# The second product of a mixture layer made to follow half a token tile behind the first, in place of a whole tile

## The chip, the core and the metric

One core of a Trainium2 chip runs the kernel. The core has TensorE (PE, with its weight loads shown apart as PEld), VectorE (DVE), ScalarE (ACT), GpSimd (POOL) and SyncE (SP, which here only issues transfers, from one queue in order). The metric is the device time of one execution in microseconds (us), lower is better; runs are compared by their median.

## The reference, cut to what matters

An attention stage makes `x`, a first gated layer (MoE 1) changes it, and the second layer (MoE 2) makes the output. Only MoE 2 is touched:

```python
def _moe2_ref(x, w_in, w_out):      # x (2304, 512), w_in (512, 2048), w_out (2048, 512)
    h = x @ w_in
    sp = np.where(h > 20.0, h, np.log1p(np.exp(np.minimum(h, 20.0))))
    g = h * np.tanh(sp)
    return (g @ w_out).astype(np.float32)
```

So there is a first product (`x @ w_in`), an elementwise function (Mish) of it, and a second product (`g @ w_out`).

## The kernel before, in words

Every operand is split into a high and a low part, so each product is made of three matmuls (high by high, high by low, low by high: lines 1644 to 1646 for the first product, 1657 to 1659 for the second).

**Tiles.** MoE 2 runs twice over the tokens, once for each half `h` of the 2048 hidden features, since only half of the weights fits. Within a half it goes over five token tiles `t`: four of 512 tokens and one with the remaining 256 (`REST`). In the half `h = 1` the tiles come in reverse. A tile has two phases, `d = 0` and `d = 1`; each takes two of the half's four quads of features, a quad being 256 features. A phase is half a tile's first product.

**A phase** (`phase`) makes seven sub-products P1 to P7 (a Strassen-like scheme), each of 12 matmuls with 256 columns (`product`), in the order 1, 5, 6, 2, 7, 3, 4. They go into four PSUM tiles: hX, hZ and one of hY0 and hY1. After P1, ACT copies hX into y (line 1781), on which P6 then accumulates. After P5, ACT copies hZ into v (line 1784). After P6, DVE adds y and v into hZ (line 1787), and only then may P7 accumulate on y. After P7, DVE adds y and v into `c22` (line 1793), and only then may P4 accumulate on y. P2, P3 and P4 are copied out by ACT (lines 1790, 1797, 1800). The results stand in two SBUF buffers, hsA (c11 and c22) and hsB (c12 and c21).

**Mish.** `mish` takes one such buffer through DVE (1664), ACT (1665), DVE (1666), ACT (1667 and 1668), DVE (1669 and 1670); `put_g` then writes the high part with ACT (1677) and the low part with DVE (1678) into `g2`. This is called the chain below; each phase has two, eA from hsA and eB from hsB. eA serves token parts and feature blocks 0 and 1 of `g2`, eB blocks 2 and 3.

**The second product** is cut into units `m2out(t, f, a)`: feature block `f` (0 to 7 of the half; 0 to 3 come from phase 0, 4 to 7 from phase 1) by token part `a` (0 to 3; 0 and 1 in `REST`). A unit is three matmuls with 512 columns, adding to the PSUM tile `po[a]`. Below "f0a2" stands for the unit with f = 0 and a = 2. f0a0 and f0a1 need eA of their phase; f0a2, f0a3, f1a0 and f1a1 need eB. After the eighth block `finish` moves `po[a]` out: in `h = 0` an ACT copy (1695) and a store to `pd`; in `h = 1` a load of `pd` into one of two buffers `r` (1700), a DVE addition (1701) and a store of the output (1703).

**Order.** The code deals the units of an earlier tile out between the products of a phase (`go(share[k])`). It is only a wish: the framework's scheduler reorders the instructions of every engine by its own estimate of when each can start. So the order that counts is that of the built program.

**Beside that** run, in `h = 0`, 16 jobs that prepare the other half's weights (POOL 190, DVE 198, 201, 205 and 231, ACT 228, stores by SP). SP also loads the next tile's `xu` (1572), the blocks of `w_out` (`load_o2`, line 1559) and the second half of `w_in`.

Of the kernel before, what the change touches and what calls it, by code (L numbers as in the profile page):

```python
# [59 lines left out]
def attn_moe_kernel(  # L60
# [14 lines left out]
    B, H, S, D = q.shape  # L75
# [17 lines left out]
    NQ = KF2 // 4  # L93
# [66 lines left out]
    for n in range(B * NU1):  # L160
        i = n % NRING
# [1317 lines left out]
    if True:  # L1479
# [21 lines left out]
        for b in range(B - 1):  # L1501
# [11 lines left out]
            if b:  # L1513
# [3 lines left out]
                    lambda i, d, b=b: park_o2((b - 1) * per + i, d), 19000.0,  # L1517
# [40 lines left out]
        def load_o2(h, j):  # L1558
            SP.dma_start(out=wo_at[j].bitcast(F32), in_=wd2[h * 8 + j].rearrange("p z f -> p (z f)"))
# [90 lines left out]
        def m2out(t, f, a):  # L1650
            q, fi = divmod(f, 2)
            T, part = divmod(a, 2)
            ts = slice(part * 128, (part + 1) * 128)
            gh, gl = (g2[:, q, BLK[fi, T] if t < B else fi, z, ts] for z in range(2))
            w = wo_at[f].rearrange("p (z f) -> p z f", z=2)
            p = po[a]
            PE.matmul(p, lhsT=gh, rhs=w[:, 0, :], start=(f == 0), stop=False)  # L1657
            PE.matmul(p, lhsT=gh, rhs=w[:, 1, :], start=False, stop=False)  # L1658
            PE.matmul(p, lhsT=gl, rhs=w[:, 0, :], start=False, stop=(f == 2 * NQ - 1))  # L1659
# [88 lines left out]
        n_y = [0]  # L1748

        def phase(t, quads, units, follow, share):  # L1750

            hsA, hsB = hs_at
# [55 lines left out]
        prev = None  # L1808
        for s, (h, t) in enumerate(order):
            after = order[s + 1] if s + 1 < len(order) else None  # L1810
            for d in range(NQ // 2):
                quads = (2 * d, 2 * d + 1)
                units = []
                if prev is not None:
                    ph, pt = prev
                    for q in quads:
                        for f in (2 * q, 2 * q + 1):
                            for a in range(4 if pt < B else 2):
                                units.append(lambda f=f, a=a, pt=pt: m2out(pt, f, a))

                def follow(i, d=d):
                    if d != NQ // 2 - 1 or after is None or after[1] == t:
                        return
                    if t < B:
                        load_x2(after[1], i)
                    elif i:
                        load_x2(after[1], 4 - i)

                n = 4 if t == REST else 7
                per = len(units) / n  # L1830
                share = [round(per * (k + 1)) - round(per * k) for k in range(n)]
                if after is None:
                    share = [1] * 7
                phase(t, quads, units, follow, share)
                if after is not None and after[0] != h:
                    for q in quads:
                        load_wi(q)
                if prev is None and d == 0:
                    for j in range(2, 8):
                        load_o2(0, j)  # L1840
                if prev is not None and prev[0] != h:
                    for q in quads:
                        for f in (2 * q, 2 * q + 1):
                            load_o2(1, f)
            if prev is not None:
                for a in range(4 if prev[1] < B else 2):
                    finish(prev[0], prev[1], a)
            prev = (h, t)
        for a in range(4):
            for f in range(2 * NQ):  # L1850
                m2out(prev[1], f, a)
            finish(prev[0], prev[1], a)
        assert not side
# [37 lines left out]
```

## Time and profile before

| what | value |
|---|---|
| median of 3 runs | 1016.59 us (1015.89 to 1020.15) |
| the profiled execution's own time | 1020.45 us |
| its span, first to last instruction | 1018.6 us |
| mean granted TensorE clock, share of full speed | 0.981 |
| PE busy | 988.6 us, 97% of the span |
| DVE busy | 681.2 us, 67% |
| ACT busy | 579.0 us, 57% |
| MoE 2 in the trace | about 623 us to the end |

Busy times are sums over instructions of one engine. Matmuls are pipelined, so a record of a matmul overlaps the next one's; how long a matmul occupies TensorE is read from the distance of two starts. The profiled execution is 3.86 us slower than the median of the runs; a prediction made against its trace has to be moved to the runs' level.

### The profile page before, as it was taken

To read this page: it belongs to the slowest core of one execution; us is meant where nothing else is said; L and a number is where in the kernel's file an instruction comes from. 1 tells how busy PE (TensorE), PEld (TensorE's weight loads), DVE (VectorE), ACT (ScalarE), POOL (GpSimd) and SP (SyncE) were. 2 spreads that over 40 slices of the span, in tenths; PEclk is the share of its full clock that TensorE was granted. 3 is DMA by queue.
4 is the path that set the end of the run, shared out by engine and by line. 5 is a ranking of instruction groups with operands and counts; after the bars stand their busy time and mean duration, and the time that the engine had idled before them with its cause. 6 is when DMAs were issued, how large, how long until landed. Compare 5 with 4: busy or idle time off the path is not lost. (4 is left out here: it accounts for less than half of the span.)

```text
span 1018.6 us, 20914 instructions
## 1 busy us (share of the span) xinstructions
PE 988.6 (97%) x8188; PEld 923.3 (91%) x8188; DVE 681.2 (67%) x1034; ACT 579.0 (57%) x1292; POOL 296.3 (29%) x319
## 2 busy tenths in 40 slices
PE   9989799999999999999999999899999999999998
PEld 7889698898999999999999999798988889988986
DVE  5845776776776567765688732897888545766664
ACT  6547677656656455755545533766566454745452
POOL 5846573662412324010254311142433100000000
PEclk9689799999999999999999999999999999999999
DMA  8378765689443484442464726866758794362503
GB/s 201 105 187 220 212 207 167 212 275 300 125 152 106 125 275 129 145 125 82 161 220 138 186 92 199 307 221 239 256 211 218 297 352 126 104 200 78 157 17 129
DMA packets 159090, 184.86 MB, mean 181 GB/s; under 512 B 68368, under 2 KB 121360, under 8 KB 158480
## 3 DMA queue, kind: packets, MB, share of 16 engines
q1 hardware_dynamic: 155296, 179.87, 55.9%
q0 software_dynamic: 3696, 3.67, 1.6%
q8 instruction: 64, 1.05, 0.4%
q14 instruction: 34, 0.28, 0.1%
HBM read 132.38 MB, written 51.12 MB: 180 GB/s over the span
## 5 line engine op out<-in xcount | busy, mean ns | idle before, releaser
L1293 PE MATMUL ps_m<-R 128*128 128x288 f32 (+2 forms) x768 | 235.8, 308 | 6.0 <-ACT R L228 3.6
L1294 PE MATMUL ps_m<-R 128*128 128x288 f32 (+2 forms) x768 | 230.9, 301 | 0.0
L1295 PE MATMUL ps_m<-R 128*128 128x288 f32 (+2 forms) x768 | 230.2, 301 | 0.1
L1293 PEld LDWEIGHTS ps_m<-R 128*128 128x128 f32 x768 | 147.9, 193 | 10.3 <-ACT R L228 3.9
L1644 PE MATMUL h<-xu,R 128*128 128x256 f32 x512 | 144.6, 283 | 4.4 <-DMA xu<-x2d 1.2
L1294 PEld LDWEIGHTS ps_m<-R 128*128 128x128 f32 x768 | 147.8, 192 | 0.8 <-issue 0.8
L1295 PEld LDWEIGHTS ps_m<-R 128*128 128x128 f32 x768 | 146.8, 192 | 1.3 <-issue 0.6
L1645 PE MATMUL h<-xu,R 128*128 128x256 f32 x512 | 144.2, 282 | 0.0
L1646 PE MATMUL h<-xu,R 128*128 128x256 f32 x512 | 144.0, 282 | 0.0
L228 ACT CAST R<-d 128x512 fp32r<-128x512 f32 (+1 forms) x146 | 91.6, 636 | 60.6 <-PE ps_m L1294 21.9
L1336 PE MATMUL ps_o<-G,R 128*128 128x288 f32 x384 | 115.5, 301 | 0.0
L1657 PE MATMUL po<-wo,g 128*128 128x512 f32 x288 | 113.3, 394 | 1.5 <-ACT o L1695 1.5
L1338 PE MATMUL ps_o<-G,R 128*128 128x288 f32 x384 | 114.2, 297 | 0.0
L1340 PE MATMUL ps_o<-G,R 128*128 128x288 f32 x384 | 113.9, 297 | 0.0
L1658 PE MATMUL po<-wo,g 128*128 128x512 f32 x288 | 112.6, 391 | 0.0
L231 DVE TENSOR_TENSOR R<-d,R 128x512 fp32r<-128x512 f32 (+1 forms) x116 | 88.7, 768 | 35.7 <-ACT R L228 34.5
L1659 PE MATMUL po<-wo,g 128*128 128x512 f32 x288 | 110.5, 393 | 0.0
L1644 PEld LDWEIGHTS h<-xu,R 128*128 128x128 f32 x512 | 96.8, 189 | 9.7 <-DVE h L1787 1.2
L1645 PEld LDWEIGHTS h<-xu,R 128*128 128x128 f32 x512 | 97.0, 189 | 4.3
L190 POOL TENSOR_SCALAR rebias<-raw 128x512 f32<-128x512 f32 x32 | 56.9, 1779 | 138.0 <-DMA raw<-in_moe_w_in_dram 60.9
L1646 PEld LDWEIGHTS h<-xu,R 128*128 128x128 f32 x512 | 96.9, 190 | 0.1
L1336 PEld LDWEIGHTS ps_o<-G,R 128*128 128x128 f32 x384 | 72.7, 189 | 0.7
(173 smaller groups left out, 2000.5 us busy)
## 6 DMA issues: line engine op xcount, KB each, us to landing
d<-wd SPq DMA_DIRECT2D x54, 512.0 KB
xu<-x2d SPq DMA_DIRECT2D x45, 512.0 KB
raw<-in_moe_w_out_dram SPq DMA_DIRECT2D x28, 512.0 KB
wd<-d SPq DMA_DIRECT2D x18, 512.0 KB
raw<-in_moe_w_in_dram SPq DMA_DIRECT2D x16, 512.0 KB
wo<-wd SPq DMA_DIRECT2D x16, 512.0 KB
x2d<-G SPq DMA_DIRECT2D x28, 288.0 KB
R<-wi2d SPq DMA_DIRECT2D x4, 1792.0 KB
```

Source lines behind the costliest of these rows:

```text
L1293: PE.matmul(p[:, 0:n], lhsT=wh, rhs=xh[:, c, ts], start=(c == 0), stop=False)
L1294: PE.matmul(p[:, 0:n], lhsT=wh, rhs=xl[:, c, ts], start=False, stop=False)
L1295: PE.matmul(p[:, 0:n], lhsT=wl, rhs=xh[:, c, ts], start=False, stop=(c == KD - 1))
L1336: PE.matmul(p[:, 0:SUB], lhsT=hi[:, o:o + 128], rhs=gt[:, f, 0, ts], start=(f == 0), stop=False)
L1338: PE.matmul(p[:, 0:SUB], lhsT=hi[:, o:o + 128], rhs=gt[:, f, 1, ts], start=False, stop=False)
L1340: PE.matmul(p[:, 0:SUB], lhsT=lo[:, o:o + 128], rhs=gt[:, f, 0, ts], start=False, stop=(f == KF1 - 1))
L1644: PE.matmul(o, lhsT=wh, rhs=x[:, c, 0, :], start=(start and k == 0 and c == 0), stop=False, skip_group_check=True)
L1645: PE.matmul(o, lhsT=wh, rhs=x[:, c, 1, :], start=False, stop=False, skip_group_check=True)
L1646: PE.matmul(o, lhsT=wl, rhs=x[:, c, 0, :], start=False, stop=(c == 1), skip_group_check=True)
L1657: PE.matmul(p, lhsT=gh, rhs=w[:, 0, :], start=(f == 0), stop=False)
L1658: PE.matmul(p, lhsT=gh, rhs=w[:, 1, :], start=False, stop=False)
L1659: PE.matmul(p, lhsT=gl, rhs=w[:, 0, :], start=False, stop=(f == 2 * NQ - 1))
```

## The change

The unit list of a phase now holds the second product of the phase before it, not of the same phase of the tile before. So the blocks f0 to f3 of a tile ride with its own phase 1, and the blocks f4 to f7 with phase 0 of the next tile. What `finish` does moves with it, to after phase 0 of the next tile. The tail after the last phase has the 16 units of its own phase, where it had 32. The loads of `w_out` are asked for in other places of the code.

```diff
@@ -1810,15 +1810,17 @@
             after = order[s + 1] if s + 1 < len(order) else None
             for d in range(NQ // 2):
                 quads = (2 * d, 2 * d + 1)
-                units = []
-                if prev is not None:
-                    ph, pt = prev
-                    for q in quads:
-                        for f in (2 * q, 2 * q + 1):
-                            for a in range(4 if pt < B else 2):
-                                units.append(lambda f=f, a=a, pt=pt: m2out(pt, f, a))
+                last_h, last_t, last_d = prev if prev is not None else (None, None, None)
+                fs = range(4 * last_d, 4 * last_d + 4) if prev is not None else ()
+                units = [
+                    lambda f=f, a=a, pt=last_t: m2out(pt, f, a)
+                    for f in fs for a in range(4 if last_t < B else 2)
+                ]
 
                 def follow(i, d=d):
+                    if prev is None and i in (7, 3):
+                        for j in range(2, 4) if i == 7 else range(4, 6):
+                            load_o2(0, j)
                     if d != NQ // 2 - 1 or after is None or after[1] == t:
                         return
@@ -1829,25 +1831,24 @@
-                if after is None:
+                if after is None and d == NQ // 2 - 1:
                     share = [1] * 7
                 phase(t, quads, units, follow, share)
                 if after is not None and after[0] != h:
                     for q in quads:
                         load_wi(q)
-                if prev is None and d == 0:
-                    for j in range(2, 8):
+                if prev is None:
+                    for j in range(6, 8):
                         load_o2(0, j)
-                if prev is not None and prev[0] != h:
-                    for q in quads:
-                        for f in (2 * q, 2 * q + 1):
-                            load_o2(1, f)
-            if prev is not None:
-                for a in range(4 if prev[1] < B else 2):
-                    finish(prev[0], prev[1], a)
-            prev = (h, t)
+                if last_h == 0 and (h == 1 or (after is not None and after[0] == 1 and d == NQ // 2 - 1)):
+                    for f in fs:
+                        load_o2(1, f)
+                if last_d == NQ // 2 - 1:
+                    for a in range(4 if last_t < B else 2):
+                        finish(last_h, last_t, a)
+                prev = (h, t, d)
         for a in range(4):
-            for f in range(2 * NQ):
+            for f in range(NQ, 2 * NQ):
                 m2out(prev[1], f, a)
             finish(prev[0], prev[1], a)
```

**Where TensorE meets f0a0 of tile t = 1 in the half h = 1.** The names: h_8172 is hX, h_8175 hZ, h_8173 and h_8174 the two hY; xu5 is the operand of P5; po_8176 and po_8177 are parts 0 and 1. Before, P1 of phase 0 of the next tile (t = 0) ends and f0a0 follows whole, then P5:

```order
L1644 MATMUL h_8172<-xu1_7773,R2_6783 128x256
L1645 MATMUL h_8172<-xu1_7773,R2_6783 128x256
L1646 MATMUL h_8172<-xu1_7773,R2_6783 128x256
L1657 MATMUL po_8176<-wo0_8154,g2_8162 128x512 [waits DVE_49]
L1658 MATMUL po_8176<-wo0_8154,g2_8162 128x512
L1659 MATMUL po_8176<-wo0_8154,g2_8162 128x512
L1644 MATMUL h_8175<-xu5_7775,R2_6783 128x256 [waits DMAHW7_49,Activation_49]
L1645 MATMUL h_8175<-xu5_7775,R2_6783 128x256
```

And in the changed program, where P5 of phase 1 of tile 1 itself ends:

```order
L1644 MATMUL h_8175<-xu5_7775,R2_6783 128x256
L1645 MATMUL h_8175<-xu5_7775,R2_6783 128x256
L1646 MATMUL h_8175<-xu5_7775,R2_6783 128x256
L1657 MATMUL po_8176<-wo0_8154,g2_8162 128x512 [waits Activation_49]
L1658 MATMUL po_8176<-wo0_8154,g2_8162 128x512
L1657 MATMUL po_8177<-wo0_8154,g2_8162 128x512 [waits DVE_49]
L1658 MATMUL po_8177<-wo0_8154,g2_8162 128x512
L1644 MATMUL h_8174<-xu6_7777,R2_6783 128x256 [waits Activation_49]
L1645 MATMUL h_8174<-xu6_7777,R2_6783 128x256
```

The matmuls with the high part of `g2` now wait for ACT (line 1677 of the phase just before), and those with the low part (1659) stand behind P6 and two thirds of P2. From there the changed program goes on with P6, P2, P7, P3, P1 of the next tile, P4, and only then f0a2; 14 units follow with no other product than half of P5 among them.

**DVE, at the chain eA in a tile of h = 1**, from its first row to the addition 1787 on which P7 waits (hs0 is hsA, hs1 is hsB, o and r belong to `finish`). Before:

```order
L1664 TENSOR_SCALAR e_11024<-hs0_8149 128x1024 [waits DVE_49,Activation_49]
L1666 SCALAR_TENSOR_TENSOR e_11024<-e_11024 128x1024 [waits Activation_49]
L1701 TENSOR_TENSOR o_11095<-po_8176,r0_8152 128x512 [waits DMAHW3_49,DMAHW2_49,PE_49]
L1701 TENSOR_TENSOR o_11099<-po_8177,r1_8153 128x512 [waits DMAHW5_49,DMAHW4_49,PE_49]
L1669 SCALAR_TENSOR_TENSOR e_11024<-e_11024,hs0_8149 128x1024 [waits Activation_49]
L1670 TENSOR_TENSOR e_11024<-e_11024,l_11025 128x1024 [waits DVE_49,Activation_49]
L1664 TENSOR_SCALAR e_11084<-hs1_8150 128x1024 [waits Activation_49]
L1701 TENSOR_TENSOR o_11103<-po_8178,r0_8152 128x512 [waits DMAHW5_49,DMAHW4_49,PE_49]
L1678 TENSOR_TENSOR g2_8162<-e_11024,g2_8162 128x2x2x256 [waits PE_49,Activation_49]
L1701 TENSOR_TENSOR o_11107<-po_8179,r1_8153 128x512 [waits DMAHW7_49,DMAHW0_49]
L1666 SCALAR_TENSOR_TENSOR e_11084<-e_11084 128x1024 [waits Activation_49]
L1787 TENSOR_TENSOR h_8175<-h_8173,v_8151 128x512 [waits PE_49,Activation_49]
```

And in the changed program:

```order
L1664 TENSOR_SCALAR e_10906<-hs0_8149 128x1024 [waits DVE_49,Activation_49]
L1666 SCALAR_TENSOR_TENSOR e_10906<-e_10906 128x1024 [waits Activation_49]
L1701 TENSOR_TENSOR o_10975<-po_8176,r0_8152 128x512 [waits DMAHW5_49,DMAHW4_49,PE_49]
L1701 TENSOR_TENSOR o_10979<-po_8177,r1_8153 128x512 [waits DMAHW6_49,DMAHW0_49,PE_49]
L1669 SCALAR_TENSOR_TENSOR e_10906<-e_10906,hs0_8149 128x1024 [waits Activation_49]
L1670 TENSOR_TENSOR e_10906<-e_10906,l_10907 128x1024 [waits DVE_49,Activation_49]
L1664 TENSOR_SCALAR e_10964<-hs1_8150 128x1024 [waits Activation_49]
L1701 TENSOR_TENSOR o_10983<-po_8178,r0_8152 128x512 [waits DMAHW7_49,DMAHW6_49,PE_49]
L1701 TENSOR_TENSOR o_10987<-po_8179,r1_8153 128x512 [waits DMAHW1_49,DMAHW0_49,PE_49]
L1678 TENSOR_TENSOR g2_8162<-e_10906,g2_8162 128x2x2x256 [waits Activation_49]
L1666 SCALAR_TENSOR_TENSOR e_10964<-e_10964 128x1024 [waits Activation_49]
L1787 TENSOR_TENSOR h_8175<-h_8174,v_8151 128x512 [waits PE_49,Activation_49]
```

All four additions of `finish`, each waiting for its load of `r`, now stand ahead of the low part (1678), and the wait of 1678 for TensorE is gone.

**ACT, in the same stretch.** Before, from the first exponential of eA on:

```order
L1665 ACTIVATE e_11024<-e_11024 128x1024 [waits DVE_49]
L1797 COPY hs1_8150<-h_8175 128x512 [waits PE_49]
L1667 ACTIVATE l_11025<-e_11024 128x1024 [waits DVE_49]
L1668 ACTIVATE l_11025<-l_11025 128x1024 [waits Activation_49]
L1800 COPY hs1_8150<-h_8174 128x512 [waits PE_49]
L1781 COPY h_8173<-h_8172 128x512 [waits PE_49]
L1677 CAST g2_8162<-e_11024 128x2x2x256 [waits DVE_49]
L1665 ACTIVATE e_11084<-e_11084 128x1024 [waits DVE_49]
L1784 COPY v_8151<-h_8175 128x512 [waits PE_49]
```

And in the changed program:

```order
L1665 ACTIVATE e_10906<-e_10906 128x1024 [waits DVE_49]
L1797 COPY hs1_8150<-h_8175 128x512 [waits PE_49]
L1667 ACTIVATE l_10907<-e_10906 128x1024 [waits DVE_49]
L1668 ACTIVATE l_10907<-l_10907 128x1024 [waits Activation_49]
L1800 COPY hs1_8150<-h_8173 128x512 [waits PE_49]
L1677 CAST g2_8162<-e_10906 128x2x2x256 [waits DVE_49]
L1665 ACTIVATE e_10964<-e_10964 128x1024 [waits DVE_49]
L1781 COPY h_8174<-h_8172 128x512 [waits PE_49]
L1784 COPY v_8151<-h_8175 128x512 [waits PE_49]
```

The copy of hX into y (1781), which P6 waits for, moved behind the cast of eA and the first exponential of eB.

## Rows read from the trace of the kernel before

**Rows 1.** The page, busy time by engine and the two products' groups.

```profile
PE 988.6 (97%) x8188; PEld 923.3 (91%) x8188; DVE 681.2 (67%) x1034; ACT 579.0 (57%) x1292; POOL 296.3 (29%) x319
...
L1644 PE MATMUL h<-xu,R 128*128 128x256 f32 x512 | 144.6, 283 | 4.4 <-DMA xu<-x2d 1.2
...
L1657 PE MATMUL po<-wo,g 128*128 128x512 f32 x288 | 113.3, 394 | 1.5 <-ACT o L1695 1.5
```

**Rows 2.** Windows: length; busy of PE, PEld, DVE, ACT, POOL; clock; DMA.

```profile
623.00:645.00 22.00, 19.36 (x153) 18.36 (x152) 10.78 (x14) 10.53 (x17) 5.76 (x7) 1.00 0.95 325
645.00:691.00 46.00, 44.29 (x279) 39.81 (x279) 41.41 (x48) 31.36 (x39) 12.89 (x11) 1.00 0.75 246
...
733.00:779.00 46.00, 44.49 (x283) 39.96 (x282) 38.93 (x47) 28.43 (x38) 18.11 (x17) 1.00 0.71 225
...
908.00:950.00 42.00, 42.00 (x264) 37.84 (x263) 26.26 (x29) 21.60 (x26) 0.00 (x0) 1.00 0.43 135
...
623.00:1014.00 391.00, 384.78 (x2403) 345.67 (x2401) 272.14 (x298) 217.49 (x271) 58.60 (x54) 1.00 0.60 199
```

**Rows 3.** Waits from 620 us on: waiter, releaser: total, times, longest.

```profile
ACT o L1695 <- DMA pd<-o: 7.3, 4, 2.9
...
DVE o L1701 <- DMA r<-pd: 6.8, 4, 3.2
...
PE po L1657 <- ACT o L1695: 1.5, 1, 1.5
```

**Rows 4.** PE timeline: start, duration, line, operation.

```profile
836.06 0.40 PE L1657 MATMUL po<-wo,g 128*128 128x512 f32 x1
...
836.75 0.40 PE L1657 MATMUL po<-wo,g 128*128 128x512 f32 x1
...
859.54 0.28 PE L1644 MATMUL h<-xu,R 128*128 128x256 f32 x1
...
943.49 0.40 PE L1658 MATMUL po<-wo,g 128*128 128x512 f32 x1
...
990.55 0.28 PE L1644 MATMUL h<-xu,R 128*128 128x256 f32 x1
...
991.98 0.40 PE L1658 MATMUL po<-wo,g 128*128 128x512 f32 x1
```

**Rows 5.** DVE timeline, with the idle time before a row and its releaser.

```profile
860.12 0.69 DVE L1787 TENSOR_TENSOR h<-h,v 128x512 f32<-128x512 f32 x1
...
943.69 0.69 DVE L1793 TENSOR_TENSOR hs<-h,v 128x512 f32<-128x512 f32 x1 [3.61 <-PE h L1646]
...
953.48 1.23 DVE L1678 TENSOR_TENSOR g<-e,g 128x1024 fp32r<-128x1024 f32 x1 [0.53 <-ACT g L1677]
...
995.88 0.69 DVE L1701 TENSOR_TENSOR o<-po,r 128x512 f32<-128x512 f32 x1 [0.88 <-DMA r<-pd]
...
1003.64 1.23 DVE L1678 TENSOR_TENSOR g<-e,g 128x1024 fp32r<-128x1024 f32 x1 [1.11 <-ACT g L1677]
```

**Rows 6.** ACT timeline.

```profile
952.39 1.05 ACT L1677 CAST g<-e 128x1024 fp32r<-128x1024 f32 x1
...
992.21 0.57 ACT L1800 COPY hs<-h 128x512 f32<-128x512 f32 x1
...
1002.56 1.05 ACT L1677 CAST g<-e 128x1024 fp32r<-128x1024 f32 x1 [1.53 <-DVE e L1670]
```

**Rows 7.** SP timeline: when a transfer was issued.

```profile
667.44 0.38 SPq L178 DMA_DIRECT2D raw<-in_moe_w_in_dram  x1
...
687.57 0.60 SPq L178 DMA_DIRECT2D raw<-in_moe_w_in_dram  x1
...
992.10 0.42 SPq L1700 DMA_DIRECT2D r<-pd  x1
```

**Rows 8.** POOL timeline: the instructions that wait for those `raw` transfers.

```profile
671.23 1.55 POOL L190 TENSOR_SCALAR rebias<-raw 128x512 f32<-128x512 f32 x1 [6.54 <-DMA raw<-in_moe_w_in_dram]
...
695.09 1.54 POOL L190 TENSOR_SCALAR rebias<-raw 128x512 f32<-128x512 f32 x1 [12.55 <-DMA raw<-in_moe_w_in_dram]
```

## Prediction

> **What bounds the kernel now.** I read the page first, then windows over MoE 2, then the waits, then single instructions. The page says that TensorE is busy 97% of the span, and that MoE 2 has 512 matmuls on each of the three lines of its first product and 288 on each line of its second [rows 1]. Busy time of pipelined matmuls proves little, so I take distances between starts. A product of 12 matmuls takes 991.98 - 990.55 = 1.43 us, a unit of three 836.75 - 836.06 = 0.69 us [rows 4]. 512 x 3 / 12 = 128 products and 288 units make 128 x 1.43 + 288 x 0.69 = 382 us, and the window from 623 to 1014 us is 391 us long [rows 2]. So TensorE is idle some 9 us in MoE 2 by starts, and 391.00 - 384.78 = 6.2 us by busy time. Of these 6.2 us, 22.00 - 19.36 = 2.6 lie ahead of 645 us, 1.7 in the next window and 1.5 between 733 and 779 us; from 908 to 950 us the sum is zero [rows 2]. The clock is granted in full (1.00) in every such window. DVE is the engine next to it: 41.41 of 46 us busy in the half h = 0, 26.26 of 42 in h = 1 [rows 2].
>
> The reader is to see that the change has little to win. It takes no matmul away, and its order begins to differ only in the second tile, behind the idle time ahead of 645 us and most of that in the next window. What can go is one wait of a unit for the copy out of `po`, 1.5 us [rows 3], and 0.4 us elsewhere.
>
> **Part 1: the waits of before that may go.** The 1.5 us come from ACT, which stood behind stores to `pd` for 7.3 us in all [rows 3]. These copies stay, at a later place, where f0a0 comes after two products (2 x 1.43 us) and not one. I take the whole 1.5 off; the bounds are 0 and 1.9 (with the 0.4).
>
> **Part 2: the wait of a unit for its own phase.** Before, `g2` was a phase old when it was read; now f0a0 follows the chain eA of the phase just before. In a tile of h = 1 the changed order has, between the end of P7 and f0a0, the products P3, P4, P1, P5 and five units: 4 x 1.43 + 5 x 0.69 = 9.2 us. The chain took, from the end of P7 at 943.49 [rows 4] over DVE's addition at 943.69 [rows 5] to the end of the cast at 952.39 + 1.05 = 953.44 [rows 6], 9.95 us, and to the end of the low part at 953.48 + 1.23 = 954.71 [rows 5], 11.2 us. The high part is thus 0.8 us late by this row. The low part is not: the changed order puts it behind four more matmuls (4 x 0.23), P6 and 8 of 12 matmuls of P2, at 9.2 + 0.9 + 1.4 + 1.0 = 12.5 us. The unit f0a2 needs eB, 11.6 us to the cast (991.98 [rows 4] to 1002.56 + 1.05 [rows 6]); between P4 and f0a2 stand eight products and four units, 14.2 us. No wait there.
>
> **Part 3: what queues behind it.** Between f0a1 and f0a2 the products now run without units. P6 needs the copy into y, which on ACT moved behind the cast of eA and an exponential of eB: 9.95 + 1.05 (as long as the cast) + 0.57 (a copy, [rows 6]) = 11.6 us behind P7, where TensorE could start P6 at 10.1. That is 1.5 us, and it contains the 0.8 of part 2, since both push the same stream. P7 needs DVE's addition behind P6: before, P6 ended at 859.54 [rows 4] and the addition stood at 860.12 for 0.69 us [rows 5], done 1.27 us behind P6; P2 covers 1.43, so 0.16 is left, less than one more DVE instruction ahead of it. On DVE all four additions of `finish` now stand ahead of the low part, and the wait for `r` with them: 992.10 [rows 7] to 995.88 [rows 5], 3.8 us from issue to use. That holds up eB and the addition for P7, and DVE waited for `r` 6.8 us in all before, 3.2 at the longest [rows 3].
>
> The sequence of the changed program has seven such stretches that before has not: three around the full tiles and one at `REST` in h = 0, three in h = 1. (Two dense ones, at the start and at the first full tile of h = 1, are in both.) One costs from 0, if ACT and DVE are as early as the scheduler placed them, to 1.5 us. I take 0.5: the row of 9.95 us has a foreign copy of 0.57 us in it, ahead of the cast, that the changed order puts behind, so the chain itself is nearer to 9.4 and f0a0 waits 0.2; the copy into y is late by the rest. 7 x 0.5 = 3.5 us, bounds 0 and 10.5.
>
> **Part 4: the tail.** After the last P4 before had 18 units ahead of the first that needs eB; the changed order has 14 units and the high matmuls of two, 14 x 0.69 + 4 x 0.23 = 10.6 us. The cast was ready 11.6 us after P4 (copy at 992.21, cast at 1002.56 [rows 6]), the low part at 1003.64 + 1.23, 12.9 us [rows 5]. So up to 1.0 us. But that chain had additions of `finish` in its way, one of them waiting 0.88 us for `r` [rows 5], and they are now a phase earlier. I take 0.5, bounds 0 and 1.0. What follows the last unit is the same.
>
> **Part 5: transfers.** `xu` for the next P1 can be loaded once P1 of phase 1 is through, and the next P1 now stands five products and two units later, 8.5 us. A transfer of the same 512 KB took from 671.23 - 667.44 = 3.8 us to 695.09 - 687.57 = 7.5 us from issue to use [rows 7, 8]. It fits in both cases, so nothing is put down for it. The loads of `w_out` stand on SP in the same order as before until after the last of the first half's, and those of the second half get more time: nothing. The wait of `put_g` for TensorE falls away; no row of the waits shows one, so it wins nothing.
>
> **A rule on TensorE's room.** The weight loads are busy 345.67 of 391.00 us in MoE 2, 88% [rows 2], while the starts show products standing end to end at 1.43 us.
>
> The Trainium skill ("Perfetto Trace Analysis", section "Identifying the Most-Contended Engine") says that matmul occupancy is no measure of headroom and that the busy share of the weight loads should be used. By that rule the rest of the window, 391.00 - 345.67 = 45 us, would be open to a better order; the sum by starts has 9. The trace disagrees with the rule for this stretch: the spacing of 1.43 us is the same in dense and mixed places.
>
> **The sum.** -1.5 + 3.5 + 0.5 = +2.5 us, from -1.9 to +11.5. Against the profiled execution: 1020.45 + 2.5 = 1022.95. It stands 1020.45 - 1016.59 = 3.86 us above the median of the runs, so the runs come to 1019.1 us, a ratio of 1.0025. About 0.5%, 5.1 us, is what a measurement of this kernel can tell from no change.
>
> **The rivals.**
> *The dense stretches pay in full (slower).* Place: P6 and P7 between f0a1 and f0a2, waiting for ACT's copy into y and DVE's addition. At 1.5 us in seven stretches and 1.0 in the tail, with nothing gone, it is 1016.6 + 11.5 = 1028. It decides from (5.1 + 1.5 - 0.5) / 7 = 0.87 us a stretch. For it: DVE is 90% busy in h = 0, and it has no slack of a phase any more. Against: before ran a dense stretch around 859 us on the same copies and additions, its addition done in time [rows 4, 5].
> *The reload of `xu` is late (slower).* SP issues in order; if the load stands 2 us behind a store that waits for DVE and lands in 7.5, P1 is 1.0 us late at each of four tile ends: 1016.6 + 2.5 + 4 = 1023.1 and, with part 3 a little above my value, over the bound.
> *TensorE has room (faster).* If the 45 us in which no weights load were usable, a tenth of it, 4.5 us, with the 1.9 us of waits would already pass the bound: 1016.6 - 6.4 = 1010.2. Against it: starts show no gap to fill.
>
> **Chances.** My sum, within 0.5%: 0.69. The dense stretches 0.21 and the reload 0.05, both slower: 0.26. Faster 0.05. My case's own bounds are 1014.7 (1016.6 - 1.9) and 1021.7; to leave out no more than 2 in 10 the range goes on into the slower rival, most of the way to its 1028: 1014.5 to 1026.
>
> **What would show it.** Right: PE idle in MoE 2 by windows of 6 to 12 us; no ACT wait of 1.5 us at a unit; the last matmul within 4 us of 1014. In the table of waits, 1644 on ACT 1781 and DVE 1787 with some tenths each, and 1657 on ACT 1677 of 0.2 to 0.8. Wrong: 1644 waiting on DMA `xu`, single waits above 1.5 us, or PE with no idle time from the second tile on. What would overturn it is a chain much faster or slower in the new order of ACT and DVE than the rows of before give.

## The result, and the profile after

The changed kernel took 1026.2 us (median of 18 runs, 1018.78 to 1031.3), the kernel before 1020.47 us in 18 runs. The ratio is 1.008, with a 95% interval of 1.0052 to 1.0109, where 1.0025 was forecast: some 8 us slower and not 2.5. (It leaves disturbed runs out, and so is not that of the medians.) The median is 7.1 us above the forecast and 0.2 above the range; 3.9 of that is the level of before, which its first three runs had put at 1016.59. The profiled execution took 1021.25 us, with a span of 1019.5.

The page of the changed kernel, the rows that answer to [rows 1]:

```profile
PE 986.6 (97%) x8188; PEld 920.7 (90%) x8188; DVE 675.3 (66%) x1034; ACT 579.1 (57%) x1292; POOL 295.9 (29%) x319
...
L1644 PE MATMUL h<-xu,R 128*128 128x256 f32 x512 | 145.9, 285 | 10.9 <-DVE h L1787 4.1
...
L1657 PE MATMUL po<-wo,g 128*128 128x512 f32 x288 | 112.8, 392 | 0.0
```

The idle time at units is gone, as part 1 said, but ahead of line 1644 it grew from 4.4 to 10.9 us. Windows, as in [rows 2], two of the half h = 0 and two of h = 1:

```profile
640.00:687.00 47.00, 43.66 (x267) 38.83 (x266) 37.22 (x44) 29.82 (x38) 13.81 (x12) 1.00 0.66 223
687.00:729.00 42.00, 40.19 (x241) 36.23 (x240) 34.54 (x43) 25.75 (x33) 14.32 (x12) 0.96 0.67 228
...
862.00:904.00 42.00, 42.00 (x261) 37.78 (x261) 29.06 (x31) 22.69 (x27) 0.00 (x0) 1.00 0.35 109
904.00:946.00 42.00, 42.00 (x265) 37.95 (x265) 26.96 (x29) 21.96 (x26) 0.00 (x0) 1.00 0.42 137
```

In the two windows of h = 1 TensorE has no idle time; behind the first tile nearly all of it lies in h = 0, and one window has a granted clock of 0.96. The waits from 620 us on, as in [rows 3]:

```profile
PE h L1644 <- DVE h L1787: 4.1, 3, 1.8
...
DVE o L1701 <- DMA r<-pd: 2.9, 3, 1.2
...
PE h L1644 <- ACT hs L1766: 2.5, 2, 1.8
PE h L1644 <- DMA xu<-x2d: 1.7, 1, 1.7
PE h L1644 <- ACT h L1781: 1.2, 2, 0.7
...
ACT o L1695 <- DMA pd<-o: 1.1, 2, 0.6
```

And each of them behind the first tile, in TensorE's timeline with the first and the last matmul of MoE 2:

```profile
617.87 0.28 PE L1644 MATMUL h<-xu,R 128*128 128x256 f32 x1
...
684.63 0.38 PE L1644 MATMUL h<-xu,R 128*128 128x256 f32 x1 [0.99 <-DVE h L1787]
707.75 0.39 PE L1644 MATMUL h<-xu,R 128*128 128x256 f32 x1 [1.81 <-DVE h L1787]
747.93 0.39 PE L1644 MATMUL h<-xu,R 128*128 128x256 f32 x1 [0.56 <-ACT h L1781]
792.12 0.36 PE L1644 MATMUL h<-xu,R 128*128 128x256 f32 x1 [1.81 <-ACT hs L1766]
835.10 0.39 PE L1644 MATMUL h<-xu,R 128*128 128x256 f32 x1 [0.68 <-ACT hs L1766]
...
1014.74 0.39 PE L1659 MATMUL po<-wo,g 128*128 128x512 f32 x1
```

Counting 12 matmuls to a product gives the places. The first two are P7: in phase 1 of the second full tile (t = 1) and in phase 0 of the third (t = 2). The third is P6 in phase 0 of the fourth (t = 3). The fourth is the third product of `REST` in h = 0. The fifth is the product behind the eight of `REST` in h = 1; it is P5 of the next full tile, since the copy of hZ into v follows it:

```profile
836.85 0.57 ACT L1784 COPY v<-h 128x512 f32<-128x512 f32 x1
```

In before the two ends of MoE 2, and between them the two waits behind the first tile, are

```profile
623.94 0.28 PE L1644 MATMUL h<-xu,R 128*128 128x256 f32 x1
...
741.60 0.50 PE L1657 MATMUL po<-wo,g 128*128 128x512 f32 x1 [1.51 <-ACT o L1695]
...
787.46 0.35 PE L1644 MATMUL h<-xu,R 128*128 128x256 f32 x1 [0.36 <-DMA xu<-x2d]
...
1013.99 0.39 PE L1659 MATMUL po<-wo,g 128*128 128x512 f32 x1
```

The second of them is the third product of `REST`, too. MoE 2 went from 390.05 to 396.87 us. The program ahead of it is the same in both, but MoE 2 starts anywhere from 616.3 to 636.4 us in the eighteen profiles, so the profiles are compared over MoE 2 alone. (The expectations below name 394.96 or 395.0 us for the changed kernel, from a start read 1.9 us late; 396.87 is right.)

Where the time went can be added up for every profile of this study. "Waits" are distances of two starts beyond the usual 0.119 us (256 columns) or 0.230 us (512), counted where two starts lie about twice the usual distance apart or more; the first tile, whose order is nearly the same in all, stands apart. "Clock" is the sum of 1 minus the granted clock over windows of 1 us in MoE 2. Some 0.2 us of a row hang on how a wait inside a stretch at half clock is split between waits and clock.

| kernel | ratio to before (95%) | MoE 2 | first tile | later waits | clock | rest |
|---|---|---|---|---|---|---|
| before | 1 | 390.05 | 4.90 | 2.20 | 0 | 382.95 |
| before, second profile | | 389.22 | 5.01 | 1.45 | 0 | 382.76 |
| changed | 1.008 (1.0052 to 1.0109) | 396.87 | 5.79 | 6.93 | 1.70 | 382.45 |
| changed again | 1.008 (1.0038 to 1.0122) | 397.60 | 5.02 | 8.67 | 1.71 | 382.20 |
| h = 1 only | 1.0006 (0.9971 to 1.0042) | 391.18 | 5.16 | 3.39 | 0 | 382.62 |
| h = 0 only | 1.0033 (0.9991 to 1.0074) | 396.11 | 5.01 | 6.88 | 1.71 | 382.51 |
| eA first | 1.0128 (1.0065 to 1.019) | 399.59 | 3.00 | 10.73 | 1.71 | 384.15 |
| split on GpSimd | 1.0131 (1.0087 to 1.0176) | 405.26 | 5.00 | 13.74 | 5.13 | 381.39 |
| xu by GpSimd | 1.0061 (1.0022 to 1.01) | 395.56 | 5.35 | 7.41 | 0 | 382.81 |
| all three | 1.0107 (1.0056 to 1.0158) | 403.92 | 5.00 | 12.43 | 3.41 | 383.08 |
| before, no subtraction | 1.0105 (1.006 to 1.015) | 399.74 | 5.47 | 7.98 | 3.41 | 382.87 |
| changed, no subtraction | 1.0154 (1.0103 to 1.0204) | 402.85 | 4.99 | 11.62 | 5.12 | 381.11 |
| h = 1 with xu | 0.9971 (0.9934 to 1.0009) | 391.90 | 5.18 | 2.64 | 1.71 | 382.37 |
| four kept | 1.007 (1.0037 to 1.0103) | 401.94 | 5.17 | 9.79 | 5.10 | 381.87 |
| before, no jobs | 0.9962 (0.9924 to 0.9999) | 386.90 | 4.03 | 0 | 0 | 382.87 |
| changed, no jobs | 0.9981 (0.9948 to 1.0015) | 391.24 | 5.08 | 3.10 | 0 | 383.06 |
| raw earlier | 1.0061 (1.002 to 1.0101) | 400.10 | 6.67 | 8.09 | 3.41 | 381.94 |
| raw earlier, xu by GpSimd | 1.0067 (1.0029 to 1.0105) | 399.08 | 6.57 | 8.16 | 1.70 | 382.64 |

The rest is 381 to 384 us in all of them, the 382 that the prediction worked out from 128 products and 288 units. So what the orders differ in is waits, and the clock behind them. Changed against before: 396.87 - 390.05 = 6.8 = 0.9 (first tile) + 4.7 (later waits) + 1.7 (clock) - 0.5 (rest). The second profiles: 8.4 = 0.0 + 7.2 + 1.7 - 0.6.

### The profile page after: what moved, and what is told of

Read it like the earlier page. It is cut to its first block, busy times and chain, and to the rows that moved or that the text cites. A ratio compares the mean times of both kernels' runs of the same rounds, so it can differ in the third digit from the quotient of the medians.

```text
span 1019.5 us, 20919 instructions
## 1 busy us (share of the span) xinstructions
PE 986.6 (97%) x8188; PEld 920.7 (90%) x8188; DVE 675.3 (66%) x1034; ACT 579.1 (57%) x1292; POOL 295.9 (29%) x319
## 4 chain that ended last, share of the span: by engine, by line
PE 67%; DMA 10%; DVE 8%; ACT 7%; issue 4%; POOL 3%; SPq 1%; ACTq 0%; POOLq 0%; DVEq 0%
PE ps_m L1293 8%; PE ps_m L1295 8%; PE ps_m L1294 8%; PE po L1659 4%; PE po L1657 4%; PE po L1658 4%; PE ps_o L1336 4%; PE ps_o L1338 4%; PE ps_o L1340 4%; PE h L1644 4%; PE h L1646 3%; PE h L1645 3%; DMA raw<-in_moe_w_out_dram 2%; DMA xu<-x2d 2%; POOL d L1540 1%
## 5 line engine op out<-in xcount | busy, mean ns | idle before, releaser
L1644 PE MATMUL h<-xu,R 128*128 128x256 f32 x512 | 145.9, 285 | 10.9 <-DVE h L1787 4.1
L1657 PE MATMUL po<-wo,g 128*128 128x512 f32 x288 | 112.8, 392 | 0.0
L1658 PE MATMUL po<-wo,g 128*128 128x512 f32 x288 | 112.7, 391 | 0.0
L1659 PE MATMUL po<-wo,g 128*128 128x512 f32 x288 | 102.2, 392 | 0.0
```

Of the source, the lines that this page charges most:

```text
L1644: PE.matmul(o, lhsT=wh, rhs=x[:, c, 0, :], start=(start and k == 0 and c == 0), stop=False, skip_group_check=True)
```

## The experiments

Theory 1: the new waits, all in h = 0 and at `REST`, and a stretch at half clock behind them. Rivals: the clock's changes from run to run alone; the shorter distance itself, in h = 1 too; the late reload of `xu`.

**The changed kernel again**, nothing altered.

> The changed kernel once more, with nothing altered. Theory 1 (new waits of the first product in h = 0 and at REST, where DVE and ACT also prepare weights and no unit stands between P6 and P7, and a stretch at a granted clock of 0.50 behind one of them): MoE 2 again 394 to 396 us from its first matmul to its last, the same waits of 1.8 us at lines 1787 and 1766; if the stretch at 0.50 hangs on the wait, it stands behind the wait near 708 us again. Rival 2 (only the clock differed from run to run): MoE 2 anywhere between 390 and 396 us, other places for the stretch. Ratio 1.004 to 1.010 by theory 1, 1.000 plus or minus 0.004 by rival 2.

MoE 2 took 397.60 us, above the 394 to 396 (which hung on the misread 395), with a ratio of 1.008 as theory 1 has it. The waits for 1787 came at the same two places (1.58 and 1.19 us), those for 1781 and 1766 too. The longest, though, names another releaser, at the same product, the third of `REST`:

```profile
796.28 0.56 PE L1644 MATMUL h<-xu,R 128*128 128x256 f32 x1 [3.11 <-DMA xu<-x2d]
```

And the half clock stood behind this wait, not behind the one of 1787. So the places come again with the program; behind which wait a stretch at half clock stands differed. **The kernel before again:**

> The kernel before once more, for a second profile. Theory 1: MoE 2 again 389 to 391.5 us with no half-clock stretch in it, though the whole may differ by 10 us with the clock ahead of MoE 2. Rival 2 (the clock alone sets the difference): MoE 2 anywhere from 389 to 397 us.

389.22 us, no such stretch, and the ratios of the runs are 1.008 twice. The clock alone does not explain the difference: the changed kernel's waits of 6.9 and 8.7 us stand in both of its profiles, before's 2.2 and 1.5 in both of its own.

**Half the distance in one half of the features only.** The list of waiting phases gets a distance for each half:

```diff
+        LAG = (2, 1)        # and (1, 2)
...
+                now = [p for p in pend if p[0] <= n_p]
...
+                pend.append((n_p + LAG[h], h, t, d))
```

> The second product follows half a tile behind only in h = 1, a whole tile in h = 0. Theory 1: the costly waits are all in h = 0 and at REST, so MoE 2 is 388 to 391 us (before 390.05, changed 394.96), a ratio of 0.997 to 1.002, and no single wait above 1.7 us behind the first tile. Rival 3 (the shorter distance itself pays, by the chain to eA and the copies of finish, in h = 1 and in the tail as well): MoE 2 392 to 394 us. Rival 2 (clock alone): nothing to be told from before.

> The second product follows half a tile behind only in h = 0, a whole tile in h = 1. Theory 1: all of the cost is here, MoE 2 394 to 396 us and a ratio of 1.003 to 1.009, with the waits at 1787 and 1766 of 1.8 us. Rival 3: half of it, 392 to 393 us. Rival 2: 390 us with other clocks.

391.18 and 396.11 us, each within 0.2 us of theory 1's range: by the profiles the cost is in h = 0. The runs say less, 1.0006 and 1.0033, the second with an interval that holds 1. In h = 1 the three dense stretches wait for nothing, and with h = 1 only nothing was paid in the tail.

**Units that need only eA first.** The eight units that need eA alone go ahead of the eight that need eB.

```diff
+            us = [(f, a) for f in range(4 * d, 4 * d + 4) for a in range(na)]
+            if na == 4:
+                us.sort(key=lambda u: (u[0] % 2) != (u[1] // 2))
```

> The changed kernel with the 16 units of a phase in another order: the eight that need only eA come first, the eight that need eB behind them, so that units stand between P6 and P7 instead of two products end to end. Theory 1, with missing cover as the cause: the new waits at 1787 in h = 0 (1.2 and 2.0 us start to start) and the one for the copy into y (0.7) fall to 0.3 or less, the stretch at half clock goes with them; those at REST (2.0 and 0.8) stay: MoE 2 390 to 391.5 us, ratio 0.999 to 1.003. If instead DVE is late by more than a unit covers (weight preparation ahead of line 1787), the waits stay above 0.8 and MoE 2 is 393 to 395 us.

The waits for 1787 in the full tiles went, as cover would have it, but MoE 2 was 399.59 us, outside either case. Other waits came in their place (1788 is the copy into y, 1684 the cast of the chain, in this kernel's lines), and with the one for xu, 3.30 us, a stretch at half clock:

```profile
734.26 0.39 PE L1644 MATMUL h<-xu,R 128*128 128x256 f32 x1 [1.19 <-ACT h L1788]
...
756.93 0.50 PE L1664 MATMUL po<-wo,g 128*128 128x512 f32 x1 [1.01 <-ACT g L1684]
...
855.16 0.50 PE L1664 MATMUL po<-wo,g 128*128 128x512 f32 x1 [1.62 <-ACT g L1684]
```

In the tail, too, a unit now waited for the cast, 1.42 us at 1025.50. So cover takes the waits at 1787 away in this order, and waits for the chain come in their place; missing cover alone is not the cause of the loss.

**The xu of REST.** It comes in 24 small transfers of 64 KB, eight of them for the third operand, which can't start before P3 of the last full tile. SP's rows of the changed kernel:

```profile
782.12 0.38 SPq L178 DMA_DIRECT2D raw<-in_moe_w_in_dram  x1
782.60 3.22 SPq L1581 DMA_DIRECT2D xu<-x2d  x5
785.91 0.56 SPq L1476 DMA_DIRECT2D wd<-hi  x1
786.52 0.52 SPq L1581 DMA_DIRECT2D xu<-x2d  x1
787.14 0.60 SPq L1477 DMA_DIRECT2D wd<-d  x1
787.78 2.39 SPq L1581 DMA_DIRECT2D xu<-x2d  x2
```

From the first to the last of the eight issues SP takes 787.78 + 2.39 - 782.60 = 7.6 us, with two stores among them. The product could have started at 790.03 + 0.12 = 790.15 (the start of the matmul ahead, and its 0.119), just when the last was issued, and starts at 792.12. Four of the eight to GpSimd:

```diff
-                            queue.dma_start(
+                            (POOL if i == 3 and b > 1 else queue).dma_start(
```

> The changed kernel with four of the eight transfers that load the third operand of REST (xu3) issued by GpSimd and not by SP. Theory 4 (the reload of xu is late at REST, since SP needs 5 to 7 us to issue eight small transfers after P3 of the last full tile and the changed order has two products fewer in between): the wait at the third product of REST falls from 1.8 (3.1 in the second profile) to 0.5 us or less, MoE 2 1.5 to 3 us shorter than the changed kernel's. Rival (that wait is for the copy into hsA at line 1766, as the changed kernel's row names it): it stays at 1.8 us and names line 1766.

The wait is gone, whatever engine the changed kernel's row names: the window holds no idle time, where the changed kernel has 55.19 of 57 us busy from 775 to 832. MoE 2 took 395.56 us, 1.3 and 2.0 less than the two profiles of the changed kernel.

```profile
775.00:832.00 57.00, 57.00 (x349) 51.01 (x348) 36.47 (x42) 29.88 (x39) 15.59 (x15) 1.00 0.85 292
```

The waits for 1787 stayed (1.21 and 2.11 us). Theory 4 holds for this one place, since the other waits stand at the same products as in the changed kernel.

**Less work for DVE.** Why is 1787 late? DVE's rows of the changed kernel ahead of the two waits:

```profile
682.74 1.23 DVE L1669 SCALAR_TENSOR_TENSOR e<-e,hs 128x1024 f32<-128x1024 f32 x1 [0.75 <-ACT l L1667]
683.88 0.69 DVE L1787 TENSOR_TENSOR h<-h,v 128x512 f32<-128x512 f32 x1
...
705.93 0.43 DVE L198 TENSOR_SCALAR d<-rebias 128x512 int32<-128x512 int32 x1 [1.43 <-POOL rebias L190]
706.39 0.69 DVE L201 SCALAR_TENSOR_TENSOR d<-raw,d 128x512 int32<-128x512 int32 x1
707.00 0.69 DVE L1787 TENSOR_TENSOR h<-h,v 128x512 f32<-128x512 f32 x1
```

In both, 1787 stands behind an instruction that itself waits, once for ACT's part of the chain, once for GpSimd's part of a weight job. First try: the jobs' subtraction (231) moved to GpSimd.

```diff
-            split(d, hi.bitcast(F32R), d.bitcast(F32R), DVE, late=True)
+            split(d, hi.bitcast(F32R), d.bitcast(F32R), POOL, late=True)
```

> The changed kernel with one kind of instruction of the weight preparation in h = 0 moved from DVE to GpSimd (the subtraction that makes the low part). Theory 1 (the addition 1787 is late because DVE also prepares weights): the two waits of TensorE for 1787 in h = 0, 1.0 to 1.8 us each in the changed kernel, fall below 0.4, and the half-clock stretch behind them goes; the wait near 790 us, at the third product of REST, stays at 2 to 3.3 us. MoE 2 390.5 to 393 us against 395.0 and 397.6 of the two profiles of the changed kernel. Rival 3 (missing cover between P6 and P7 by itself): the waits stay above 0.8 us and MoE 2 is 394 to 397 us.

MoE 2 took 405.26 us. The waits for 1787 went (0.48 and the first tile's left), but the chain became late: TensorE waited for `g2` (1.9 us) and the copies. The work went from DVE to GpSimd, and some of DVE's other instructions became longer (the last section says which); the mean in ns, changed kernel first, then this one (1670 is 1673 in it):

```profile
L1670 DVE TENSOR_TENSOR e<-e,l 128x1024 f32<-128x1024 f32 x17 | 21.2, 1246 | 1.9 <-ACT l L1668 1.5
...
L198 DVE TENSOR_SCALAR d<-rebias 128x512 int32<-128x512 int32 x16 | 7.2, 453 | 6.6 <-POOL rebias L190 6.6
```

```profile
L1673 DVE TENSOR_TENSOR e<-e,l 128x1024 f32<-128x1024 f32 x18 | 25.9, 1439 | 5.2 <-ACT l L1671 4.6
...
L198 DVE TENSOR_SCALAR d<-rebias 128x512 int32<-128x512 int32 x16 | 14.4, 898 | 15.2 <-POOL rebias L190 15.2
```

**All three** (this, xu by GpSimd, and `REST` alternating between hsA and hsB):

> Both of these together, and REST alternating between hsA and hsB. If the waits at 1787, at xu and at 1766 with the half-clock stretch are the whole loss, MoE 2 comes to 387 to 390 us, at or below before's 390.05, and the ratio to 0.994 to 1.001. If half the distance costs by itself something that these three don't hold, MoE 2 stays above 392 us.

403.92 us, with the same late chain, and the third product of `REST` waited again: 2.39 us, for which its row names the cast of the chain (1677, 1680 in it). The wait of 0.68 us for 1766 (1772 in it) stood unchanged at 841.66, so one buffer hsA is not its cause.

Second try: the subtraction left out, in both kernels.

```diff
+        if late and leave_out[0]:
+            return z
         return eng.tensor_tensor(out=lo, in0=src, in1=hi.bitcast(F32), op=ALU.subtract)
```

> The changed kernel without the DVE subtraction that makes the low part of the weights prepared in h = 0 (16 instructions, 14.2 us of DVE; the second half's weights are therefore not the reference's). GpSimd gets no more work, unlike in the run before. Theory 1 (DVE is late with the addition 1787 because it also prepares weights): the waits of TensorE for 1787 in h = 0 fall from 1.0 to 1.6 and 1.2 to 2.1 us to 0.4 or less, the wait near 790 us for xu stays at 2 to 3 us; MoE 2 391 to 394 us. Rival 3 (nothing but the missing cover between P6 and P7): waits stay above 0.8 us.

> The kernel before without the same subtraction. Theory 1: before has units between P2 and P7, its additions are in time already, so nothing is won but part of its one wait for the copy out of po (1.5 and 0.7 us): MoE 2 388 to 390 us. If DVE's load costs before as much as it costs the changed kernel, MoE 2 falls by 3 us or more, to 387 us or less.

Both expectations failed: with 14 us less of DVE's work the changed kernel took 402.85 and before 399.74 us. The scheduler placed what was left in another order, the waits for 1787 (1792 in it) stayed at 1.23 and 1.55 us, and at `REST` TensorE waited 4.59 us for `xu`, in before 3.09 at the same product (there the row names a store to `pd`). So less work on DVE alone does not take the waits away. As the order is another too, the runs don't show that the work has no part in them.

**No weight jobs in h = 0.** Zeros are stored in their place, and the streams of DVE, ACT and GpSimd are rid of them. The 16 loads of raw weights leave SP's queue with them, so the runs take jobs and loads away together.

```diff
-            side.append([lambda k=k: side_narrow(k)])
-            side.append([lambda k=k: side_sums(k)])
+            side += [[], [], [lambda k=k: side_zero(k)]]
```

> The changed kernel without the 16 jobs that prepare the second half's weights in h = 0; zeros are stored in their place by as many transfers, so the output holds the first half's part alone. If the jobs in the streams of DVE, ACT and GpSimd are what makes the waits behind the first tile: h = 0 is then like h = 1, where the same dense stretches cost nothing, no wait at 1787 or 1781 above 0.4 us, and MoE 2 385 to 389 us. If the dense order costs by itself: waits at 1787 above 0.8 us remain and MoE 2 is 391 us or more.

> The kernel before without the same jobs. By the first theory before and changed are now alike: MoE 2 385 to 389 us, within 1.5 us of the changed kernel without the jobs. If the shorter distance costs by itself, before is 3 us or more shorter.

In the full tiles of h = 0 the changed kernel now has the last quarter of P2 and then P7, P3, P1 and P4 end to end twice (from 726.39 and from 768.52 us) and no wait; a window of it over the first:

```profile
719.62:772.00 52.38, 52.38 (x346) 48.03 (x345) 33.16 (x34) 31.52 (x42) 0.00 (x0) 1.00 0.40 115
```

The first half of the expectation holds in h = 0: no wait for 1787 or 1781 in any tile but the first (one of 0.66 us for 1781 stands where the full tiles of h = 1 begin). The second fails: before is 386.90 us, with no wait behind the first tile, the changed kernel 391.24, outside its 385 to 389. Of the 4.3 us between them 1.0 lie in the first tile (most at `xu`), the rest where `REST` ends and h = 1 begins, above all at a unit that waits for its own phase's chain:

```profile
837.50 0.50 PE L1657 MATMUL po<-wo,g 128*128 128x512 f32 x1 [1.55 <-ACT g L1677]
```

The 4.3 us are what the expectation gave as the sign of a shorter distance that costs by itself, but the runs don't bear them out: they put the two at 0.9981 and 0.9962 of before, with intervals that overlap, and their medians 1.2 us apart (1018.15 and 1016.95). With the jobs before and changed differ by 8 us.

**Raw weights asked for one job earlier**, with two buffers.

```diff
-            if k + 1 < len(jobs):
-                side_load(k + 1)
+            side_load(k + 2)
```

> The changed kernel with two buffers for the raw weights, so that each job's transfer is asked for one job earlier (one of the two buffers r, used in h = 1 alone, shares its place with a buffer of the jobs). If DVE 198 waits for GpSimd because that transfer is late: GpSimd's waits for raw fall from 47 us in h = 0 to under 15, the wait of 1.8 us at 707 (1.2 and 2.1 in the other profiles) goes, the ones near 684 (behind the chain) and at REST (xu) stay; MoE 2 392 to 395 us. If not: waits at 1787 as before, MoE 2 395 to 398 us.

> The same with four of the eight transfers of xu3 for REST issued by GpSimd. Both causes together would take MoE 2 to 389.5 to 393 us, a ratio of 0.998 to 1.005; below 0.995 only if the earlier transfers also take the first tile's waits away.

GpSimd's waits for that transfer fell as expected, from 46.9 + 6.7 to 11.0 us; in the changed kernel, and then with two buffers, both from 620 us on:

```profile
POOL rebias L190 <- DMA raw<-in_moe_w_in_dram: 46.9, 6, 9.1
...
PE h L1644 <- DVE h L1787: 4.1, 3, 1.8
```

```profile
POOL rebias L191 <- DMA raw<-in_moe_w_out_dram: 11.0, 1, 11.0
...
PE h L1645 <- DVE h L1791: 6.8, 3, 2.9
```

TensorE's waits for 1787 (1791 in it) rose all the same, to two of 2.9 us and one of 1.0 in the first tile; ahead of the two long ones, DVE has three and four instructions of jobs and chain in a row, the first of which waits for ACT (1.01 and 1.87 us). MoE 2 took 400.10 us, and 399.08 with xu by GpSimd. So an earlier transfer does not take the waits away either, in an order that again is another.

**Two tries for a better kernel.** Four of 16 units kept for the next phase, in the full tiles of h = 0:

```diff
+                later = [u for u in todo if u[0] % 4 > 1 and u[1] > 1] if h == 0 and t < B and last_t is not None else []
```

> The changed kernel, with four of the 16 units of a phase in the full tiles of h = 0 kept for the phase after, where the code asks for them between P6 and P7; parts 0 and 1 come ahead of parts 2 and 3. Missing cover as the cause: with units ready at any time the waits at 1787 in h = 0 fall to 0.5 us or less and MoE 2 is 391 to 394 us. If the scheduler uses the kept units up ahead of P6, the waits stay above 0.8 us and MoE 2 is at 394 to 398 us, as in the changed kernel.

The scheduler used them ahead of P6, as the second case says, but MoE 2 took 401.94 us and not 394 to 398, with waits of 3.43 and 2.03 for 1787 (1792 in it). And h = 1 only, with xu by GpSimd:

> The half-tile distance in h = 1 alone, with four of the eight transfers of xu3 for REST issued by GpSimd: the best that the runs so far point to. By theory 1 the wait for xu at REST (0.6 us here) goes and the waits behind the first tile add up to 1 to 3 us, as in before: MoE 2 388.5 to 391 us, ratio 0.997 to 1.002, no gain that can be told.

391.90 us, 0.9971 (0.9934 to 1.0009): the wait for xu at `REST` is gone, and no gain can be told. No kernel of this study that does its whole work is faster than before beyond doubt.

## Why the prediction was wrong

The sum of the prediction, beside what the two profiles of each kernel give, in us. Waits are distances of two starts beyond the usual, as in the table of runs, so they are a little longer than the idle times of the rows.

| step of the prediction | forecast | measured, first profiles | second profiles |
|---|---|---|---|
| part 1, the unit's wait for 1695 goes | -1.5 | -1.67 | -0.85 |
| part 3, seven dense stretches | +3.5 | +3.84 | +4.54 |
| part 4, the tail | +0.5 | +0.28 | 0 |
| part 5, `xu`: the third product of `REST` | 0 | +1.97 - 0.53 = 1.44 | +3.27 - 0.59 = 2.68 |
| in no part: P5 behind `REST` in h = 1 | 0 | +0.83 | +0.83 |
| in no part: the clock | 0 | +1.70 | +1.71 |
| first tile and rest | 0 | +0.39 | -0.55 |
| sum | +2.5 | +6.8 | +8.4 |

- **Reading of before:** right. TensorE had little idle time to give, by starts, and the rest of 381 to 384 us in eighteen orders is its working of 382. (DVE's 90% is one window of h = 0; from 660 to 830 us it was busy 131.56 of 170 us, 77%.) The rule of the Trainium skill on the weight loads' busy share ("Perfetto Trace Analysis", "Identifying the Most-Contended Engine"), by which the prediction had 45 us open, got no support from any of the orders.
- **Part 1:** right. The wait of a unit for 1695 is gone from the changed kernel, and is there in both profiles of before (1.51 and 0.69 us) and in h = 1 only (1.46).
- **Part 2:** the wait of 0.2 us for the cast (0.8 by its row) did not show: in a full tile no unit of the changed kernel waited for the chain. It looked at no `REST`: there such a wait exists (0.91 us with xu by GpSimd, 1.55 without jobs), though not in the two profiles of the changed kernel.
- **Part 3: right in its sum by luck, wrong in its price.** It saw the mechanism, P6 and P7 waiting for 1781 and 1787 in stretches without units, but gave all seven stretches one price, 0.5 us, from a chain in a tile of h = 1. The three in h = 1 cost 0, and so did the one at `REST`, but for its `xu`. The three in the full tiles of h = 0 cost 0.72 to 1.97 us each. There the weight jobs stand in the same streams, and 1787 waits behind instructions that wait for ACT or GpSimd. That the jobs, with their loads, make these waits is shown: without them dense stretches in the same tiles cost nothing. Which of the jobs' waits does it is not: neither less work, nor GpSimd, nor an earlier transfer helped, and each gave another order.
- **Part 4:** 0.5 us for the tail, of which 0.28 showed in one profile, in the last phase, and nothing in the other.
- **Part 5 is the step that failed.** It put nothing down for the reload of `xu`, since one transfer of 512 KB, a whole full tile's, fits by its time from issue to use. `REST` has eight small ones for one operand, and SP is 7.6 us from the first to the last issue. TensorE waited 1.81 and 3.11 us there, 0.4 in before, and the wait went when GpSimd issued four of the eight. The rival of the reload was real, though at the third product of `REST`, not at the first product of four tiles.
- **The clock, at nothing without a reason:** a stretch at half clock stood behind one of the long waits in both profiles of the changed kernel, 1.7 us each time, and none in the two of before. With part 5 it makes 3.1 of the 4.3 us that the sum misses in the first profiles, and 4.4 of 5.9 in the second. Most of what is left is the wait of P5 behind `REST`, for which nothing is shown but that a second buffer hsA leaves it as it is.

**Open:** which wait of the jobs makes 1787 late; why the changed kernel without jobs still took 4.3 us more than before in one profile (by runs it can't be told); and when a wait brings the clock down.

## What to carry to other kernels

Price a stretch in each place by the streams of that place: ask what else stands on DVE and ACT there, and for whom that waits, and not only how busy they are. Where a scheduler makes the order, an edit that takes work away can cost some 10 us (before without the subtraction: 399.74 and not 390.05), since the rest is dealt out anew; so compare waits place by place, and don't read a cause from one edited kernel. Count a load by its number of issues, too, when one queue issues them in order.

## What the runs showed of the hardware

**Half clock behind a wait.** In the changed kernel, some 1.5 us behind the wait that ended at 707.75 us, TensorE's granted clock goes from 1.00 (2.4 GHz) to 0.50 (1.2 GHz) and back; windows of 1 us:

```profile
708.00:709.00 1.00, 1.00 (x10) 1.00 (x10) 1.00 (x2) 0.00 (x0) 0.63 (x1) 1.00 0.86 242
709.00:710.00 1.00, 1.00 (x8) 1.00 (x7) 0.92 (x2) 0.00 (x0) 1.00 (x2) 0.65 0.72 283
710.00:711.00 1.00, 1.00 (x7) 1.00 (x7) 1.00 (x2) 0.00 (x0) 0.92 (x3) 0.50 0.00 0
711.00:712.00 1.00, 1.00 (x6) 1.00 (x6) 1.00 (x2) 0.00 (x0) 1.00 (x2) 0.50 0.00 0
712.00:713.00 1.00, 1.00 (x8) 1.00 (x7) 0.54 (x2) 1.00 (x2) 1.00 (x1) 0.65 0.00 0
713.00:714.00 1.00, 1.00 (x10) 1.00 (x10) 1.00 (x2) 1.00 (x2) 0.92 (x1) 1.00 0.23 93
```

Its matmuls stand 0.213 us apart there, in place of 0.119. The sum over the stretch is 1.7 us, and the kernel pays it on top of the wait. In the eighteen profiles 28 waits of TensorE in MoE 2 lasted 1.8 us or more; with 19 of them such a stretch came at their end or within 3 us, and none stood in MoE 2 without one of them. An equal wait at 792.12 in the changed kernel, with the same 1.81 us, had none.

**DVE beside GpSimd.** With the subtraction on GpSimd, DVE's 198 took 898 ns in the mean and not 453, and the chain's product 1439 and not 1246; DVE's busy time from 640 to 832 us rose from 139.99 to 146.31 us although 14.2 us of work had left it. The means hide two kinds. Thirteen instructions of DVE that read SBUF alone began in that stretch while a 231 ran on GpSimd. Each ended a fixed time behind GpSimd's, however early it had begun: four 198 by 0.28 us (2.32 to 2.34 us long, where the other twelve took 0.41 to 0.43), two 1664 by 0.55, and seven of the chain's 1666, 1669 and 1670 by 1.08. Those that had begun ahead of the 231 kept their usual time, and so did two 1793, which read PSUM as well. One of the 198:

```profile
680.24 2.12 POOL L231 TENSOR_TENSOR d<-d,hi 128x896 fp32r<-128x896 f32 x1
```

```profile
680.30 2.34 DVE L198 TENSOR_SCALAR d<-rebias 128x512 int32<-128x512 int32 x1 [2.80 <-POOL rebias L190]
```

The Trainium skill ("SBUF — State Buffer", "SBUF: two separate sides") says that the two engines share a pair of ports, and that for some kinds of instruction whichever starts first holds it for its whole instruction while the other waits; these rows agree.
